# Splitting the next group's x earlier in the last second layer, and turning the keys right behind a unit's result

## The chip, the cores and the metric

The kernel runs on one core of a Trainium2 chip. The metric is the device time of one execution in microseconds (us); the time of the kernel before is 1023.07 us, the median of three runs from 1022.1 to 1024.09.

## The reference

Two blocks run one after the other. The first is a gated linear recurrence over 4 batches, 8 heads, 768 positions and head dimension 48; its output, with the heads side by side, is the input x of a mixture of 4 experts:

```
state = alpha[t] * state + k[t] v[t]^T          # per batch and head, 48 x 48
y[t]  = q[t] state
x = y, (4 * 768) x (8 * 48)                     # 3072 rows of 384
p = domain_probs / (sum of domain_probs + 1e-9)
out = sum over e of p[:, e] * (max(x @ w1[e], 0) @ w2[e])     # w1: 384 x 1024, w2: 1024 x 384
```

## The kernel before

**Units and groups.** A unit is one chunk of 128 positions of one batch: 6 chunks times 4 batches, 24 units. The recurrence of a unit is a generator, `attention(u)`, with 17 steps (counted here from 0). The units' outputs are gathered into groups of rows for the experts: group 0 has 2 units, groups 1 to 5 have 4 each, group 6 the last 2. Units 2 to 5 make group 1, 6 to 9 group 2, 10 to 13 group 3, 14 to 17 group 4, 18 to 21 group 5.

**The MoE.** For each group and expert, `up` (the first layer, called 8 times, once for each 128 columns of the hidden layer) and then `down` (the second layer). From group 1 on, a product of float32 numbers is made from three parts of each operand (in the code: top, low and dif), so that `up` of one column block takes 9 matmuls of 128x512 (L775) and `down` of a full group 96 matmuls of 128x384 (L852). These 96 steps go through two of the parts first (64 steps) and then through the third part slot by slot, a slot being one unit's 128 rows. When a slot's last matmul has been issued, `add_up` adds its PSUM result into an SBUF accumulator (L880 on ACT for the first expert, L882 on DVE for the others). The PSUM tiles of `up` ("one") and of `down` ("ops") share one tag, g, with four buffers.

**The parts of x.** ACT copies a unit's output from PSUM into `x_raw` (L675). During the last `down` of a group, `split_x` makes the parts of the next group's x: its step 0 makes the top part on ACT (L734), its steps 1 to 3 make low (L271) and dif (L805) on DVE for one third of the 384 input columns each. `down` runs these four steps from the list `between`, each when its matmul index has reached a given share of the steps. `split_x` for the two-unit group 6 runs in group 5's first expert, in smaller pieces.

**The hidden parts.** `up` makes the top hidden part on ACT (L777) and the low one on DVE (L800); `down` makes dif (L805) at every fifth step, eight times.

**The order.** All is issued by hand, in one program order, and each engine works through its own instructions in that order. Attention steps are dealt out between the matmuls of the MoE: `deal` gives each unit a stretch of a planner's clock, `BEATS` or `IN_PAIRS` (units 11 to 17) say at which share of the stretch each of the 17 steps falls, and `advance` runs the steps that are due while `up` and `down` count the clock up by `cost`. Two units are always in progress. For units in pairs, `TOGETHER` puts step 15 of a unit at the time of step 7 of the next one, and step 16 at step 11. Step 7 makes the score products (L567, tiles of 128x64).

**The end of a unit.** From unit 2 on, step 14 is `turn_keys`: four PE transposes of the last key tile into a PSUM tile (L287, called from L683) and an ACT copy into the tile AT (L683). It does nothing for the last chunk of a batch, units 20 to 23. Step 15 is `result`: PE products into a PSUM tile "yps" (L662, column strips of 32) and the ACT copy L675. Step 16 multiplies the turned keys by the values (L697) and updates the state on DVE (L707, L708). The key tiles of all units come from one pool with five buffers; the PSUM tiles of the transposes, of the result and of the state product share one tag, w, with two buffers. From unit 10 on, the inputs a, k and q are transposed on DVE (L488) instead of PE, so that the transposes L287 of these units are those of `turn_keys` alone.

Of the kernel before, what the change touches and what calls it, by code (L numbers as in the profile page):

```python
# [20 lines left out]
def kernel(  # L21
# [94 lines left out]
    half = B // 2  # L116
# [47 lines left out]
    in_runs = 10  # L164
# [10 lines left out]
    def load(u, names):  # L175
        if u >= len(units):
            return
        cb, b = units[u]
        for nm in names:
            src = srcs[nm][b, :, cb * P:(cb + 1) * P, :].rearrange("h s d -> s h d")  # L180
            if u == in_runs and nm != "v":
                nc.gpsimd.memset(runs_of[nm][:, :, RUN - HD // 4:], 0.0)
            for g in range(P // QUAD if u >= in_runs and nm != "v" else 0):
                i, tail = divmod(g, 2)
                off, n = (QUAD, RUN - HD // 4) if tail else (0, RUN)
                runs = srcs[nm][b].rearrange("(a i) s d -> i a (s d)", i=2)[
                    i, :, cb * P * D:(cb + 1) * P * D].rearrange("a (t n) -> t a n", t=QUAD)
                nc.sync.dma_start(out=runs_of[nm][QUAD * g:QUAD * (g + 1), :, :n],
                                  in_=runs[:, :, off:off + n])
            if u >= in_runs and nm == "a":  # L190
                continue
            nc.sync.dma_start(out=raw(u, nm)[:, :, :D], in_=src)
# [13 lines left out]
    def load_piece(l, i, beside=False):  # L206
        if i >= E * NQ * LAST:
            return
        gi, k = divmod(i, E * NQ)
        e, c = divmod(k, NQ)  # L210
        if gi > l and not (l == 1 and fresh(gi, e)):
            w = wt[l][i] = wts.tile([P, 3, KC * QF], F32R, name=f"w{l + 1}",
                                    bufs=AHEAD if l == 0 else NQ)
            nc.sync.dma_start(out=w.bitcast(F32), in_=kept[l][k])
            return
        if l == 1 and gi == 0 and not beside:
            return
        if l == 0:

            if e == 0:  # L220
                shared[c] = wts.tile([P, 3, KC * QF], F32R, name="w2", bufs=NQ)
            w = shared[c][:, 2 - e % 2].bitcast(F32)
        else:

            if gi > 1 or gi == 1 and e > 0:
                if c == 0:
                    shared["w2"] = hid.tile([P, NQ, KC * QF], F32, name="hT", bufs=NQ)
                w = shared["w2"][:, c]
            else:
                w = hidden[c][:, gi].rearrange("p f n -> p (f n)")[:, :KC * QF].bitcast(F32)  # L230
        wt[l][i] = w
        if l == 0:
            nc.sync.dma_start(
                out=w.rearrange("p (c f) -> p c f", f=QF),
                in_=moe_w1[e].rearrange("(c p) f -> p c f", p=P)[:, :, c * QF:(c + 1) * QF])
        else:
            nc.sync.dma_start(
                out=w.rearrange("p (c d) -> p c d", d=DM),
                in_=moe_w2[e].rearrange("(c p) d -> p c d", p=P)[:, c * FPQ:(c + 1) * FPQ])
# [34 lines left out]
    def norm_probs():  # L274
        nc.vector.reduce_sum(out=tot, in_=p_all, axis=AX.X)
        nc.vector.tensor_scalar_add(out=tot, in0=tot, scalar1=1e-9)
        nc.vector.reciprocal(out=tot, in_=tot)
        nc.vector.tensor_mul(p_all, p_all, tot.unsqueeze(2).broadcast_to([P, NBLK, E]))
# [197 lines left out]
    def attention(u):  # L476
# [206 lines left out]
                nc.scalar.copy(out=AT, in_=turned(lambda p: KT[:, p, :]))  # L683


        for step in (turn_keys, result) if u >= half else (result, turn_keys):
            step()
            yield

# [30 lines left out]
    def split_x(gi, step):  # L720

        n = len(groups[gi]) * P
        if step == 0 and gi < LAST:
            xTs[gi] = work.tile([P, 3, KC, NT], F32R, name="xT", bufs=1)
        elif step == 0:

            xTs[gi] = [work.tile([P, NP, P], F32R, name="KT", bufs=5) for _ in range(5)]
        for kc in range(KC) if step == 0 else [step - 1]:
            parts = [x_part(gi, part, kc) for part in range(3)]
            pieces = [(xraws[gi][:, kc, :n], parts)] if gi < LAST else                 [(raw[:, kc, :], [part[:, s * P:(s + 1) * P] for part in parts])  # L730
                 for s, raw in enumerate(xraws[gi])]
            for x, out in pieces:
                if step == 0:
                    nc.scalar.activation(out=out[0], in_=x, func=ACT.Copy, scale=TRIM)  # L734
                else:
                    split_rest(x, out)
# [159 lines left out]
    def cost(layer, gi, e):  # L896
        n = len(groups[gi]) / 4
        if layer == 0:
            return 2.1 * n if gi > 0 else 2.6 * n
        return 4.1 if gi > 0 else 5.4  # L900
# [50 lines left out]
    def advance(spent):  # L951
        nonlocal clock
        clock += spent
        while waiting and clock >= waiting[0][0]:
            next(waiting.popleft()[2], None)

    with tc.manual_schedule():
        nc.scalar.dma_start(out=ident_all, in_=nc.inline_tensor(ident_np, name="ident_c").ap())
        nc.scalar.dma_start(out=masks_all, in_=nc.inline_tensor(mask_np, name="masks_c").ap())
        nc.gpsimd.memset(sts[B - 1], 0.0)  # L960
        for nm in "akq":
            for r in (early[nm], apart[nm]):
                nc.gpsimd.memset(r[:, :, D:], 0.0)
        nc.gpsimd.memset(lat[HALF:, :, :HALF], 0.0)
        for t in values + blocks:
            nc.gpsimd.memset(t, 0.0)
        for t in sts[:-1]:
            nc.gpsimd.memset(t, 0.0)

        load(0, "aqkv")  # L970
        load(1, "akqv")
        for i in range(NQ):
            load_piece(0, i)

        idle = ps.tile([P, DM], F32, name="idle", tag="g", bufs=4)
        zeros = sts[B - 1].rearrange("p a i d -> p (a i d)")

        def fill(times, n=P):  # L980
            for _ in range(times):
                nc.tensor.matmul(idle[:, :n], lhsT=zeros[:, :P], rhs=zeros[:, :n], start=True, stop=True)

        runs = [None, attention(1)]
        fill(7)
        runs[0] = first_unit(fill, runs[1])
        nc.sync.dma_start(out=p_all, in_=moe_domain_probs.rearrange("(n p) e -> p n e", p=P))

        span = cost(0, 0, 0) * FCH / 2 + cost(1, 0, 0)
        waiting.extend((span * (k + 1) / 15, u, runs[u])  # L990
                       for k, u in enumerate([1, 1, 1, 0, 1, 0, *[1] * 8]))
        for fc in range(FCH):
            up(0, 0, fc, slice(0, 1))
            if fc == FCH // 2:
                norm_probs()
            advance(cost(0, 0, 0) / 2)
        down(0, 0, [0], deque())
        while waiting:
            next(waiting.popleft()[2], None)
        clock = 0.0  # L1000
        waiting.extend((1.0 + k, 1, runs[1]) for k in range(2))
        waiting.extend(deal())

        for (gi, e), after in zip(tasks, [*tasks[1:], (None, None)]):
            rest = gi == e == 0
            for fc in range(FCH):
                up(gi, e, fc, slice(1, len(groups[0])) if rest else None)
                advance(cost(0, gi, e) / (2 if rest else 1))
            each = len(groups[gi]) if gi > 0 else 1
            turns = [range(k, k + each) for k in range(rest, len(groups[gi]), each)]  # L1010
            for k, slots in enumerate(turns):

                between = deque()
                if after[1] == 0:

                    for step, at in enumerate((0.0, 0.3, 0.42, 0.54) if gi == 0 else
                                              (0.0, 0.6, 0.7, 0.78)):
                        at = at * len(turns) - k
                        if 0 <= at < 1:
                            between.append((at, lambda step=step: split_x(after[0], step)))  # L1020
                down(gi, e, slots, between)
        while stores:
            stores.popleft()()
# [28 lines left out]
```

## Time and profile before

The profiled execution took 1022.68 us, of which 1020.8 us are the span that the profile covers.

| what | before |
|---|---|
| median of three runs | 1023.07 us |
| the profiled execution | 1022.68 us, span 1020.8 us, mean granted clock 0.994 |
| L852, second layer, 2112 matmuls | 377.8 us busy |
| L775, first layer, 1440 matmuls of 128x512 | 344.3 us busy |
| L271 and L805 on xT, 15 each | 10.3 and 10.4 us busy |
| L683, copies of turned keys, 19 | 11.1 us busy, 582 ns each |
| L882, sums of a slot, 66 | 39.7 us busy |

The last second layers of groups 1 to 5 begin, by the timeline of PE, at 309.08, 474.97, 632.31, 796.95 and 833.58 us from the start of the span, and the next group's first layer begins at 330.15, 492.06, 651.93, 815.32 and 850.22 us. (That of group 5 is that of its first expert.)

How to read the profile: times count from the start of the span. A row of a timeline gives the start, the length, the engine, the line, the operation, what is written and read, the shape and the number of instructions merged into it, and in brackets how long the engine was idle before it and what ended that. A row of waits gives the waiting engine and line, what it waited for, the sum, the number and the longest. A row of busy times by stretch gives for each engine the busy time and the number of instructions, then the granted share of the TensorE clock (PEclk) and the DMA load. A chain lists the pieces of work that released one another, in order of time.

### The profile page before, as it was taken

What the parts mean: (1) busy time and instruction counts of PE and PEld (TensorE: products, weight loads), DVE (VectorE), ACT (ScalarE), POOL (GpSimd) and SP (SyncE); (2) the same over time, 40 slices, a digit from 0 to 9 for tenths busy, and PEclk for the clock granted to TensorE, in tenths of its full rate; (3) what the DMA queues carried; (4) which work ended last, traced back from release to release, by engine and by line L of the source; (5) the groups of instructions that cost most, each with busy time, mean ns of one, the idle gap of its engine ahead of it and who ended that gap; (6) DMA issues with size and microseconds to landing.
All of it is one profiled execution on the core that took longest, in us unless ns stands there. A gap on an engine that the chain in (4) does not pass through costs nothing.

```text
span 1020.8 us, 21134 instructions
## 1 busy us (share of the span) xinstructions
PE 998.8 (98%) x8564; PEld 888.5 (87%) x8564; DVE 701.0 (69%) x1430; ACT 438.5 (43%) x961; POOL 36.1 (4%) x79
## 2 busy tenths in 40 slices
PE   8889999999999999999999999999999999999998
PEld 7767777989888799898898898898988989899998
DVE  5698869676999768677767666886786742434333
ACT  4677765364354444335443415444454232111111
POOL 2010000000000100000000000000000000000000
PEclk9999999999999999999999999999999999999999
DMA  9499699478989799789889759887796445453531
GB/s 209 132 383 292 201 317 356 152 285 279 348 292 293 279 298 329 292 248 321 287 259 339 230 216 376 271 283 286 211 368 238 165 200 190 182 204 167 226 146 47
DMA packets 155632, 260.19 MB, mean 255 GB/s; under 512 B 95216, under 2 KB 132464, under 8 KB 133520
## 3 DMA queue, kind: packets, MB, share of 16 engines
q1 hardware_dynamic: 149072, 216.44, 63.6%
q0 software_dynamic: 6016, 42.08, 10.2%
q8 instruction: 68, 1.11, 0.4%
q10 hardware_dynamic: 448, 0.33, 0.1%
q14 instruction: 28, 0.23, 0.1%
HBM read 216.35 MB, written 42.47 MB: 254 GB/s over the span
## 4 chain that ended last, share of the span: by engine, by line
PE 83%; DVE 11%; ACT 3%; issue 2%; DMA 0%; SPq 0%; DVEq 0%; ACTq 0%
PE ops L852 35%; PE one L775 32%; PE sc L567 5%; PE yps L662 3%; PE one L769 2%; PE tp L287 2%; DVE w L252 1%; ACT qb L541 1%; DVE hT L800 1%; PE sps L697 1%; DVE QT L548 1%; DVE near L577 1%; DVE w L253 1%; PE far L623 1%; DVE hT L805 1%
## 5 line engine op out<-in xcount | busy, mean ns | idle before, releaser
L852 PE MATMUL ops<-w,hT 128*128 128x384 f32 x2112 | 377.8, 338 | 1.2 <-DVE hT L800 1.2
L852 PEld LDWEIGHTS ops<-w,hT 128*128 128x128 f32 x2112 | 365.2, 188 | 4.5 <-DVE hT L800 2.0
L775 PE MATMUL one<-xT,w 128*128 128x512 f32 x1440 | 344.3, 395 | 3.7 <-DVE acc L882 3.6
L775 PEld LDWEIGHTS one<-xT,w 128*128 128x128 f32 x1440 | 267.7, 188 | 62.0 <-DVE acc L882 4.6
L777 ACT ACTIVATE hT<-one 128x512 fp32r<-128x512 f32 (+1 forms) x192 | 108.0, 562 | 342.2 <-PE one L775 325.2
L800 DVE SCALAR_TENSOR_TENSOR hT<-one,hT 128x512 fp32r<-128x512 f32 (+1 forms) x192 | 122.0, 644 | 101.9 <-ACT hT L777 101.6
L541 ACT COPY qb<-QT 64x256 f32<-64x256 f32 x322 | 131.2, 407 | 98.3 <-DVE QT L518 45.0
L548 DVE TENSOR_TENSOR QT<-QT,AT 128x256 f32<-128x256 f32 x158 | 66.5, 421 | 79.2 <-ACT qb L541 78.2
L805 DVE SCALAR_TENSOR_TENSOR hT<-hT 128x512 fp32r<-128x512 f32 (+1 forms) x192 | 111.7, 639 | 0.1
L577 DVE COPY_PREDICATED near<-masks,sc 128x256 f32<-128x256 uint8 x138 | 73.8, 535 | 43.7 <-PE sc L567 40.4
L567 PEld LDWEIGHTS sc<-qb,KT 128*64 128x64 f32 x2208 | 69.7, 138 | 7.9 <-issue 6.3
L567 PE MATMUL sc<-qb,KT 128*64 128x64 f32 x2208 | 74.0, 223 | 1.5 <-ACT qb L541 0.8
L882 DVE SCALAR_TENSOR_TENSOR acc<-ops,p_all,acc 128x384 f32<-128x384 f32 x66 | 39.7, 614 | 42.2 <-PE ops L852 42.2
L560 DVE TENSOR_TENSOR KT<-KT,AT 128x256 f32<-128x256 f32 x161 | 67.4, 419 | 1.6 <-PE sc L567 1.6
L559 ACT COPY KT<-KT 128x256 f32<-128x256 f32 x138 | 57.4, 416 | 3.4
L769 PE MATMUL one<-xT,w 128*128 128x256 f32 (+1 forms) x240 | 47.4, 346 | 0.4 <-ACT xT L460 0.4
L852 PE MATMUL ops<-hT 128*128 128x384 f32 x128 | 46.2, 494 | 0.0
L769 PEld LDWEIGHTS one<-xT,w 128*128 128x128 f32 x240 | 38.5, 194 | 5.2 <-ACT xT L460 0.6
L550 DVE TENSOR_TENSOR AT<-AT 128x256 f32<-128x256 f32 (+1 forms) x138 | 39.2, 284 | 4.7
L891 POOL DMA_DIRECT2D out_dram<-acc x22 | 11.9, 541 | 675.7 <-DVE acc L882 675.7
L775 PE MATMUL one<-KT,w 128*128 128x256 f32 x288 | 34.6, 279 | 0.0
L662 PE MATMUL yps<-lat,rv 128*32 128x128 f32 x736 | 33.1, 273 | 1.4 <-ACT lat L640 1.4
(119 smaller groups left out, 711.8 us busy)
## 6 DMA issues: line engine op xcount, KB each, us to landing
w<-kept SPq DMA_DIRECT2D x140, 1152.0 KB, 8.7
kept<-w POOLq DMA_DIRECT2D x32, 1152.0 KB, 9.1
hT<-in_moe_w_dram SPq DMA_DIRECT2D x36, 384.0 KB, 5.8
w<-in_moe_w_dram SPq DMA_DIRECT2D x16, 384.0 KB, 6.1
rv<-in_v_dram SPq DMA_DIRECT2D x24, 192.0 KB, 9.0
out_dram<-acc POOLq DMA_DIRECT2D x22, 192.0 KB, 5.8
rk<-in_k_dram SPq DMA_DIRECT2D x14, 192.0 KB, 6.1
rq<-in_q_dram SPq DMA_DIRECT2D x14, 192.0 KB, 3.0
```

What stands on the lines that cost most here:

```text
L541: nc.scalar.copy(out=qb[rows, :, i, :].rearrange("p a (b r) -> p a b r", r=m), in_=qv[rows])
L548: nc.vector.tensor_mul(qv, qv, spread(dv[:, :, :, 0], m))
L560: nc.vector.tensor_mul(new[:, :, :, 0, :], old[:, :, :, 0, :], spread(halved(decs[li])[:, :, :, 1], m))
L567: nc.tensor.matmul(out[HALF * s:HALF * (s + 1), 2 * p:2 * p + 2, :], lhsT=KTs[li][:, p, HALF * s:HALF * (s + 1)], rhs=qbs[li][:, p, :, QUA ...
L577: nc.vector.copy_predicated(near.rearrange("p a (b two r) -> p a b two r", two=2, r=m)[:, :, :, 1, :], mk.unsqueeze(1).broadcast_to([P, H, ...
L662: nc.tensor.matmul(yps[QUAD * j:QUAD * (j + 1), c, :], lhsT=lhsT, rhs=rhs, start=begins, stop=ends)
L769: nc.tensor.matmul(one, lhsT=w[:, kc], rhs=xraws[gi][:, kc, lo:hi], start=(kc == 0), stop=(kc == KC - 1))
L775: nc.tensor.matmul(one, lhsT=w[:, part, kc], rhs=x_part(gi, part, kc), start=(part == 1 and kc == 0), stop=(part == 0 and kc == KC - 1))
L777: nc.scalar.activation(out=parts[0], in_=one, func=ACT.Relu, scale=TRIM)
L800: nc.vector.scalar_tensor_tensor(out=low, in0=x, scalar=0.0, in1=top.bitcast(F32), op0=ALU.max, op1=ALU.subtract)
L805: nc.vector.scalar_tensor_tensor(out=dif, in0=low.bitcast(F32), scalar=-4096.0, in1=top.bitcast(F32), op0=ALU.mult, op1=ALU.add)
L852: nc.tensor.matmul(sums[slot], lhsT=h, rhs=w, start=(n == begins[slot]), stop=(n == ends[slot]))
```

## The change

Two things change. The list of shares at which the steps of `split_x` run in the last `down` goes from 0.0, 0.6, 0.7, 0.78 to 0.0, 0.42, 0.5, 0.58 for every group but group 0, whose shares stay. And from unit 10 on (`in_runs` is 10), step 14 does nothing, and step 15 runs `result` and then `turn_keys` in one go; units before the tenth keep their order. The number of steps and their times stay. For units 20 to 23 nothing changes, since `turn_keys` does nothing there and `result` stays in step 15.

```diff
@@ attention @@
-        for step in (turn_keys, result) if u >= half else (result, turn_keys):
+        joined = u >= in_runs
+        if joined:
+            yield
+            result()
+        for step in (turn_keys,) if joined else (turn_keys, result) if u >= half else (result, turn_keys):
             step()
             yield
@@ the loop over tasks @@
                     for step, at in enumerate((0.0, 0.3, 0.42, 0.54) if gi == 0 else
-                                              (0.0, 0.6, 0.7, 0.78)):
+                                              (0.0, 0.42, 0.5, 0.58)):
                         at = at * len(turns) - k
                         if 0 <= at < 1:
                             between.append((at, lambda step=step: split_x(after[0], step)))
```

## The prediction

> **What bounds the kernel.** I read the page first, then the waits of PE, the busy time and granted clock by stretch around the last second layer of each group, the chain of waits there, and the timelines of DVE, ACT and PE.
>
> ```profile
> PE 998.8 (98%) x8564; PEld 888.5 (87%) x8564; DVE 701.0 (69%) x1430; ACT 438.5 (43%) x961; POOL 36.1 (4%) x79
> ```
>
> PE is the bound over the span: whatever makes it stand longer, or gives it more to do, is added to the end. DVE has slack on average only. The waits of PE name where it stands:
>
> ```profile
> engine line waited for: us in total, times, longest us
> PE one L775 <- DVE acc L882: 3.6, 2, 2.5
> ...
> PE ops L852 <- DVE hT L800: 1.2, 2, 1.0
> ```
>
> The first two waits stand where one group ends and the next begins: 2.54 us before 330.15 (group 1 to 2) and 1.10 us before 651.93 (group 3 to 4). There the first matmul of the next first layer needs a PSUM buffer of tag g that the sum of slot 0 (L882, on DVE) still reads. The long one has a sequel:
>
> ```profile
> core 0: us, PE busy (x) PEld busy (x) DVE busy (x) ACT busy (x) POOL busy (x), PEclk, DMA share, GB/s
> ...
> 326.20:329.60 3.40, 1.41 (x9) 1.09 (x7) 3.30 (x8) 1.57 (x4) 0.00 (x0) 1.00 0.97 238
> 329.60:333.00 3.40, 2.85 (x7) 2.27 (x8) 3.22 (x7) 0.00 (x0) 2.04 (x4) 0.50 1.03 378
> ...
> 650.45:653.85 3.40, 2.30 (x11) 1.34 (x10) 3.33 (x7) 1.33 (x3) 0.54 (x1) 1.00 0.88 314
> ```
>
> After a stretch of 3.40 us with PE busy for 1.41 (58% idle) the clock is halved for the next 3.4 us; a stretch with 32% idle, the third row, leaves it whole. The half clock costs (333.00 - 330.15) / 2 = 1.43 us. The clock records of this trace change only at multiples of 3.413 us from each other; stretches on that raster with 58 and 60% idle lost the clock, one with 50% kept it (an early one, among transposes, lost it with 42%). I take 1.85 us idle inside one stretch as the point.
>
> **Part 1, the x parts earlier.** A last second layer has 96 matmul steps. The three pairs of split instructions (L271, then L805) move from steps 58, 68 and 75 to 41, 48 and 56 (0.6, 0.7, 0.78 and 0.42, 0.5, 0.58 of 96, rounded up). They stay on DVE; no instruction is added, and no DMA moves. What counts is what they now stand ahead of in DVE's queue: the sum of slot 0, issued behind step 71 in groups 2 to 5 (64 steps of parts 0 and 1, then 8 for a slot) and behind step 77 in group 1 (where two of a slot's eight come first for all slots). So in group 1 all three pairs are ahead of it both before and after; in groups 2, 3 and 4 the third pair stood behind it and now stands ahead. One pair takes 1.32 us (491.42 to 492.74 below).
>
> *Group 3 to 4.* The chain runs through DVE without a break:
>
> ```profile
> 650.02 0.61 DVE xT L271
> 650.64 0.02 issue
> 650.66 0.69 DVE xT L805
> 651.35 0.54 DVE acc L882
> 651.89 0.04 issue
> 651.93 2.30 PE one L775 x8
> ```
>
> DVE is busy for 17.68 of the 18.06 us from 633.84 to 651.90 (its busy time by stretch), so nothing absorbs the pair: L882 ends 1.32 later, PE starts at 653.25. Before, PE then lost some 0.2 us on the third pair (x part 1 of the last third is the third matmul's input); that goes. Net +1.1 us, and the wait grows from 1.10 to 2.42.
>
> *Group 2 to 3.* No wait before; the DVE and PE timelines show how narrow it is:
>
> ```profile
> 489.56 0.68 DVE L271 TENSOR_TENSOR xT<-x_raw,xT 128x512 fp32r<-128x512 f32 x1
> 490.28 0.69 DVE L805 SCALAR_TENSOR_TENSOR xT<-xT 128x512 fp32r<-128x512 f32 x1
> 490.89 0.61 DVE L882 SCALAR_TENSOR_TENSOR acc<-ops,p_all,acc 128x384 f32<-128x384 f32 x1
> 491.42 0.68 DVE L271 TENSOR_TENSOR xT<-x_raw,xT 128x512 fp32r<-128x512 f32 x1
> 492.13 0.69 DVE L805 SCALAR_TENSOR_TENSOR xT<-xT 128x512 fp32r<-128x512 f32 x1
> 492.74 0.61 DVE L882 SCALAR_TENSOR_TENSOR acc<-ops,p_all,acc 128x384 f32<-128x384 f32 x1
> ```
>
> ```profile
> 485.89 0.60 PE L287 MATMUL tp<-ident,KT 128*128 128x128 f32 x4
> 486.25 5.97 PE L852 MATMUL ops<-w,hT 128*128 128x384 f32 x33
> 492.06 2.24 PE L775 MATMUL one<-xT,w 128*128 128x512 f32 x9
> ```
>
> L882 of slot 0 ends at 491.50, PE wants its buffer at 492.06. With the third pair ahead it ends at 492.82 (DVE is busy for 15.95 of the 16.26 us from 475.80 to 492.06), so PE starts 0.8 later. Part 2 also takes unit 14's four transposes out of this layer: PE comes 0.45 sooner, only to wait 1.25 instead.
>
> *Group 1 to 2.* The same instructions stand ahead of slot 0's sum, and DVE is busy for 20.56 of 20.90 us (309.20 to 330.10): wait and half clock stay. *Group 4 to 5:* L882 would end at 813.8, PE wants it at 815.32: nothing. *Group 5 to 6:* DVE is idle from 843 to 852: nothing.
>
> Earlier splits make attention steps of DVE (copies into QT, KT, the masked takes) up to 4 us later. Who waits for them are ACT's copies (2.7 to 8.4 us idle ahead of the next L777) and the products and results of the next first layer, 2 us or more later: nothing. If that cover were gone, each would cost what is missing of 1.3 us.
>
> **Part 2, turns behind the result.** Only units 10 to 19 turn keys at all (20 to 23 are last chunks). Four transposes inside matmuls of the MoE cost PE 0.45 us: 96 steps with them took 492.06 - 474.97 = 17.09, without 850.22 - 833.58 = 16.64. So there is no cost of interruption to save; the work just moves.
> - Units 10, 17 and 19 get matmuls of the MoE behind the turns. Starts in the trace: 0.20 us from the result's last matmul to the next full-width one, 3 x 0.109 inside the transposes, 0.03 from there to the MoE, and 0.09 extra on the second matmul, where a return from a result costs 0.11. Added 0.33, removed 0.45: -0.12 each.
> - Units 11 to 16 and 18 get the next unit's products, of 128x64 tiles, right behind. Result to products takes 0.20; now result to transposes 0.20, inside 0.33, and transposes to products, which the trace does not show: between 0.03 (to a full-width matmul) and 0.22 (to the first unit's 64x32 tiles); I take 0.20, measured to L458's small tiles, the nearest. Added 0.53, removed 0.45: +0.08 each, with ends of -0.1 and +0.1.
> - Sum: 7 x 0.08 - 3 x 0.12 = +0.2. Of unit 14's removed 0.45 nothing is gained, as shown: +0.45.
>
> On ACT the copy of the turned keys (582 ns) now stands ahead of the next unit's L559; behind them the next L777 had waited 3.50 us for PE in the joint turn at 536 to 540, which hides it. On DVE the KT write of the next unit (L560) comes to wait for the transposes, since it takes over the buffer that they read; DVE stood there 5.29 us for the products anyway. The state update that needs the turned keys is at least one first-layer chunk (2.1 us) later. Each would cost up to 0.6 us a unit without that cover.
>
> One gain: unit 10's copy (582 ns, starting 339.35) leaves ACT's queue ahead of the qb copy for which DVE waits 3.73 us until 340.67. DVE then runs unbroken to PE's wait of 1.03 us for L800 at 356.98. DVE 0.47 earlier: -0.47, less the -0.12 of unit 10, which is then hidden.
>
> **Sum.** 2 to 3: +0.8 +0.45; 3 to 4: +1.1; turns +0.3 (unit 10's gain now hidden); wait at 357: -0.47. Together +2.2 us. Then the clock: a 2.42 us wait puts at least 1.85 us into one stretch of 3.41 for (3.41 - 1.85 + 2.42 - 1.85) / 3.41 = 62% of its positions. That is the likelier, and by the row at 330 costs 1.4: +3.6. The profiled execution took 1022.68 us (span 1020.8 and 1.9 around it), 0.4 below the median of 1023.07; 1022.68 + 3.6 = **1026.3 us**.
>
> **Rivals.**
> - *The clock stays whole* (27%): all as above without the drop, 1024.9. For it: 38% of the positions, and the wait may come out shorter. The Trainium skill, "TensorE: Matmul & The Clock Gate", HAM oscillation, says that idle gaps over some 3.4 us bring the clock down; by it 2.42 us are harmless and the sum would be this one. The row at 330, half clock after 2.54 us, speaks against the rule as it stands.
> - *DVE absorbs the pair* (15%): if L882 slips by 0.6 or less, group 2 to 3 loses nothing, 3 to 4 at most 0.6, and the turns near 0: 1023.2. Against it: 0.3 to 0.4 us idle in both stretches.
> - *Faster* (10%): the place is 327.6 to 333.0. Splits started sooner let DVE reach slot 0's sum at least 0.7 us sooner there (its busy time would have to hold hidden waiting); from there the wait falls under 1.85 and the half clock goes: -0.7 - 1.43, down to -4.0 for all, and the other two borders lose nothing for the same reason: 1018.7 to 1020.5. Against it: the same queue ahead, 98% busy.
> - *The change does nothing* is part of the second rival: were the third pair to land behind the sum still, only the turns would be left.
>
> My forecast has 48%. Runs of this kernel can tell 0.2%, some 2.05 us, from no change. Slower by more: nearly all of the forecast (46) and 16 of the first rival's 27, 62%; within: the rest, 28%; faster: 10%. The range runs from 1022.7 (second rival with its turns at their low end) to 1027.6 (the forecast, turns at their high end, a whole half-clock stretch of 1.7): it leaves out the faster case and little above.
>
> **What would show it.** Right: L882 after three split pairs at the end of groups 2 and 3; PE's wait for it near 1.2 us at group 2 to 3 and 2.4 at 3 to 4; a stretch at half clock behind the latter; an unchanged wait of 2.5 at 1 to 2; the wait for L800 near 0.6. Wrong: DVE idle in those stretches, or a wait at 1 to 2 that has shrunk.

## The result and the profile after

The changed kernel takes 1026.35 us, the median of six runs from 1024.74 to 1028.93; the kernel before took 1022.59 us in six runs beside them (1020.8 to 1024.13). The ratio is 1.0038 with a 95% interval from 1.002 to 1.0057: 3.8 us slower. The profiled execution took 1025.26 us with a span of 1023.4. Four lines were added, so L775 is now L779, L800 L804, L805 L809, L852 L856 and L882 L886.

PE has the same work as before, to 0.2 us, in a span 2.6 us longer (page, busy time of the changed kernel):

```profile
PE 998.6 (98%) x8564; PEld 887.2 (87%) x8564; DVE 701.9 (69%) x1430; ACT 439.3 (43%) x961; POOL 36.1 (4%) x79
```

The waits of PE say where it stood (waiting line, releaser, sum, number, longest):

```profile
engine line waited for: us in total, times, longest us
PE one L779 <- DVE acc L886: 6.0, 3, 2.5
...
PE ops L856 <- DVE hT L804: 0.8, 2, 0.6
```

Three waits for a slot's sum in place of two, 6.0 us in place of 3.6. DVE's timeline at the border of group 2 to 3 shows the cause:

```profile
489.63 0.69 DVE L271 TENSOR_TENSOR xT<-x_raw,xT 128x512 fp32r<-128x512 f32 x1
490.35 0.69 DVE L809 SCALAR_TENSOR_TENSOR xT<-xT 128x512 fp32r<-128x512 f32 x1
490.96 0.42 DVE L548 TENSOR_TENSOR QT<-QT,AT 128x256 f32<-128x256 f32 x1
...
491.94 1.14 DVE L886 SCALAR_TENSOR_TENSOR acc<-ops,p_all,acc 128x384 f32<-128x384 f32 x2
```

The third split pair (489.63) now stands ahead of slot 0's sum; before, it stood behind that sum and ahead of slot 1's (rows 490.89 to 492.74 in the prediction). With nothing left between them, the two sums show as one row, 491.94. (The attention step at 490.96 stood ahead of slot 0's sum before, too.) PE's timeline has the answer at all three borders, each row with the idle time ahead of it:

```profile
329.32 3.87 PE L779 MATMUL one<-xT,w 128*128 128x512 f32 x9 [2.52 <-DVE acc L886]
...
492.61 2.34 PE L779 MATMUL one<-xT,w 128*128 128x512 f32 x9 [1.10 <-DVE acc L886]
...
654.71 5.51 PE L779 MATMUL one<-xT,w 128*128 128x512 f32 x23 [2.42 <-DVE acc L886]
```

The wait is 2.5 us as before at 1 to 2, 1.10 where there was none at 2 to 3, and 2.42 in place of 1.10 at 3 to 4.

The two profiles must be laid side by side with care. The profile of before had a half-clock stretch at 15.6 us, long before anything differs, and the one after had not: the changed kernel is 0.82 us ahead when it reaches the change and 2.61 behind from 718 us on. The change cost 3.43 us in this profile, without any drop of the clock at 3 to 4.

### The profile page after: what moved, and what is told of

Its sections match the earlier page's. It is cut to its first block, busy times and chain, and to the rows that moved or that the text cites. A ratio compares the mean times of both kernels' runs of the same rounds, so it can differ in the third digit from the quotient of the medians.

```text
span 1023.4 us, 21133 instructions
## 1 busy us (share of the span) xinstructions
PE 998.6 (98%) x8564; PEld 887.2 (87%) x8564; DVE 701.9 (69%) x1430; ACT 439.3 (43%) x961; POOL 36.1 (4%) x79
## 4 chain that ended last, share of the span: by engine, by line
PE 80%; DVE 13%; ACT 3%; issue 3%; DMA 0%; SPq 0%; DVEq 0%; ACTq 0%
PE ops L856 33%; PE one L779 32%; PE sc L567 5%; PE yps L662 3%; PE one L773 2%; PE tp L287 2%; DVE hT L809 2%; DVE w L252 1%; DVE hT L804 1%; ACT qb L541 1%; DVE QT L548 1%; PE sps L701 1%; DVE near L577 1%; PE far L623 1%; DVE w L253 1%
## 5 line engine op out<-in xcount | busy, mean ns | idle before, releaser
L856 PE MATMUL ops<-w,hT 128*128 128x384 f32 x2112 | 376.0, 337 | 1.0 <-DVE hT L804 0.8
L856 PEld LDWEIGHTS ops<-w,hT 128*128 128x128 f32 x2112 | 365.5, 188 | 4.5 <-DVE hT L804 1.7
L779 PE MATMUL one<-xT,w 128*128 128x512 f32 x1440 | 343.8, 395 | 6.1 <-DVE acc L886 6.0
L779 PEld LDWEIGHTS one<-xT,w 128*128 128x128 f32 x1440 | 268.1, 189 | 63.9 <-DVE acc L886 7.3
L804 DVE SCALAR_TENSOR_TENSOR hT<-one,hT 128x512 fp32r<-128x512 f32 (+1 forms) x192 | 122.0, 645 | 101.5 <-ACT hT L781 101.1
L809 DVE SCALAR_TENSOR_TENSOR hT<-hT 128x512 fp32r<-128x512 f32 (+1 forms) x192 | 111.7, 639 | 0.1
L886 DVE SCALAR_TENSOR_TENSOR acc<-ops,p_all,acc 128x384 f32<-128x384 f32 x66 | 39.5, 614 | 41.5 <-PE ops L856 41.5
L856 PE MATMUL ops<-hT 128*128 128x384 f32 x128 | 46.2, 494 | 0.0
L779 PE MATMUL one<-KT,w 128*128 128x256 f32 x288 | 34.6, 279 | 0.0
```

The source lines that it names most:

```text
L779: nc.tensor.matmul(one, lhsT=w[:, part, kc], rhs=x_part(gi, part, kc), start=(part == 1 and kc == 0), stop=(part == 0 and kc == KC - 1))
L804: nc.vector.scalar_tensor_tensor(out=low, in0=x, scalar=0.0, in1=top.bitcast(F32), op0=ALU.max, op1=ALU.subtract)
L809: nc.vector.scalar_tensor_tensor(out=dif, in0=low.bitcast(F32), scalar=-4096.0, in1=top.bitcast(F32), op0=ALU.mult, op1=ALU.add)
L856: nc.tensor.matmul(sums[slot], lhsT=h, rhs=w, start=(n == begins[slot]), stop=(n == ends[slot]))
```

## The experiments

The theory: what costs is the place of the third split pair in DVE's queue, ahead of slot 0's sum, for which PE waits; a long wait may take the clock with it. Rival "turns": the joined turns of the keys cost most of it. Rival "earliness": earlier splits delay attention on DVE, and that costs. All edits are against the kernel before unless they say otherwise; experiments 1 to 4 ran beside 23 runs of it, median 1023.04 us, the others beside 9, median 1023.13.

**1. The split shares alone.**

```diff
-                                              (0.0, 0.6, 0.7, 0.78)):
+                                              (0.0, 0.42, 0.5, 0.58)):
```

> The split shares of the change alone; step order of the units as before. Queue theory (what costs is that the third split pair stands ahead of slot 0's sum on DVE at two group borders): the wait at group 2 to 3 is about 0.8 us (not 1.1, since unit 14's transposes are still in that layer), at 3 to 4 about 2.4, at 1 to 2 still 2.5; 2.1 us slower than before without a drop of the clock behind the 2.4 us wait, 3.5 with one, so +2 to +3.5 in the median. Rival 'turns' (the joined turns cost most of it): within 1 us of before, waits as before.

Measured: 1026.81 us, ratio 1.0042 (1.003 to 1.0054), +3.8 us. PE's timeline at 2 to 3 and 3 to 4:

```profile
494.36 1.89 PE L775 MATMUL one<-xT,w 128*128 128x512 f32 x7 [0.68 <-DVE acc L882]
655.66 1.65 PE L775 MATMUL one<-xT,w 128*128 128x512 f32 x3 [2.42 <-DVE acc L882]
```

0.68 and 2.42 us, as the theory said; the second row runs three matmuls in 1.65 us, so here the clock fell. Against the kernel before, this profile loses 0.94 us around 2 to 3, 1.32 in the wait at 3 to 4 and 1.28 in the matmuls behind it. The rival "turns" (the turns cost most of it) is refuted: none are joined here, and the loss is as large. It isn't the same loss, though. Without the clock it is 2.3 us here and 3.4 in the changed kernel, which leaves some 1.1 for the turns; the drop behind the 2.42 us wait makes up the difference in this profile. The total lies a little above the +2 to +3.5 expected; all six runs had a mean granted clock of 0.992 or 0.993, those of the changed kernel 0.992 to 0.998.

**2. The joined turns alone** (the first hunk of the change, old shares).

```diff
+        joined = u >= in_runs
+        if joined:
+            yield
+            result()
```

> The joined turns alone; split shares as before. Queue theory: no wait at 2 to 3, 1.1 us at 3 to 4, 2.5 at 1 to 2; what is left are the turns themselves, by the trace of the changed kernel +0.14 us for a unit whose turns are followed by products, some +0.4 where the wait for the hidden dif parts eats what unit 11's removal saves, -0.3 at the wait for L800: about +1 us in all. Rival 'turns': +3 us or more.

Measured: 1023.85 us, ratio 1.0004 (0.9994 to 1.0014): not told apart from before. The profile can: waits for the sums of 2.5 and 1.1 us at the same borders as before, and 1.1 us lost against the kernel before between 310 us and 718 us (1.44 to 2.53 us behind), as expected.

**3. Early pairs, third pair behind the sum.**

```diff
-                                              (0.0, 0.6, 0.7, 0.78)):
+                                              (0.0, 0.42, 0.5, 0.78)):
```

> The kernel before with the first two split pairs as early as in the change (0.42 and 0.5) and the third where it was (0.78), so behind slot 0's sum in groups 2 to 5. Queue theory: waits as before (2.5, none, 1.1), time within 0.5 us of before. Rival 'earliness' (the delay of attention's DVE steps by earlier splits is what costs): two thirds of the loss of the splits, +1.4 to +2.3 us.

Measured: 1023.45 us, ratio 1.0008 (1 to 1.0017), +0.4 us. In the profile the distance to the kernel before is 1.49 us ahead of the first of these layers and 1.51 at 750 us: two pairs moved by 17 and 20 matmuls cost nothing. "Earliness" is refuted; of the three moves, only the third one's, past the sum, costs.

**4. Third pair one slot later.** In group 1 it comes behind slot 0's sum; no other place in the order changes.

```diff
-                                              (0.0, 0.6, 0.7, 0.78)):
+                                              (0.0, 0.6, 0.7, 0.82)):
```

> The kernel before with the third pair at 0.82 instead of 0.78: on DVE this moves one pair in group 1 behind slot 0's sum, and nothing else. Queue theory: the wait at 1 to 2 falls from 2.5 to 1.2 us, so the clock stays whole there: -1.3 from the wait and -1.4 from the clock in the runs that had the drop, 2 to 2.7 us faster. Rival 'earliness': later x parts make the first layer wait for them instead, no gain or slower. Page's rule of 3.4 us idle for the clock: only the 1.3.

Measured: 1019.62 us, ratio 0.9966 (0.9953 to 0.9979): 3.4 us faster than before, with one number changed. The border of group 1 to 2 in the kernel before, DVE and PE:

```profile
328.15 0.68 DVE L271 TENSOR_TENSOR xT<-x_raw,xT 128x512 fp32r<-128x512 f32 x1
328.87 0.69 DVE L805 SCALAR_TENSOR_TENSOR xT<-xT 128x512 fp32r<-128x512 f32 x1
329.48 1.14 DVE L882 SCALAR_TENSOR_TENSOR acc<-ops,p_all,acc 128x384 f32<-128x384 f32 x2
...
330.15 3.65 PE L775 MATMUL one<-xT,w 128*128 128x512 f32 x9 [2.54 <-DVE acc L882]
```

DVE's timeline there with the third pair later:

```profile
326.76 0.69 DVE L805 SCALAR_TENSOR_TENSOR xT<-xT 128x512 fp32r<-128x512 f32 x1
327.37 0.61 DVE L882 SCALAR_TENSOR_TENSOR acc<-ops,p_all,acc 128x384 f32<-128x384 f32 x1
327.90 0.68 DVE L271 TENSOR_TENSOR xT<-x_raw,xT 128x512 fp32r<-128x512 f32 x1
328.61 0.69 DVE L805 SCALAR_TENSOR_TENSOR xT<-xT 128x512 fp32r<-128x512 f32 x1
```

PE's, at the same place:

```profile
328.03 2.52 PE L775 MATMUL one<-xT,w 128*128 128x512 f32 x9 [1.19 <-DVE acc L882]
```

The sum (327.37) now precedes the third pair, the wait falls from 2.5 to 1.19 us, and nine matmuls take 2.52 us in place of 3.65: the half-clock stretch is gone. Against the kernel before the profile gains 1.34 in the wait and 1.13 in the nine matmuls behind it, 2.5 us in all, within the 2 to 2.7 expected. The 3.4 us between the medians are more; their interval reaches from 2.1 to 4.8, and the rest isn't traced to a cause. (In this profile the clock also stayed whole at 67 us, far ahead of the edit, where the profile of before lost it.) The later pair is in time for PE.

**5. Two pairs behind the sum, top part first.**

```diff
+            parts_in_order = (0, 1, 2) if fc == 0 and e == 0 else (1, 2, 0)
-            for part in (1, 2, 0):
+            for part in parts_in_order:
...
-                                              (0.0, 0.6, 0.7, 0.78)):
+                                              (0.0, 0.6, 0.82, 0.82)):
```

> The kernel before with the second and third pair both at 0.82, which puts two pairs behind slot 0's sum at every border; and, since they then come late, the first block of an expert-0 first layer takes the top part of x first, then low and dif. Queue theory: no wait for slot 0's sum at 1 to 2 and 3 to 4 (one pair less each than in the kernel with 0.82 for the third alone); some 0.6 to 1 us of waiting for xT or for slot 1's sum in its place at 1 to 2, 0.5 at 3 to 4; 3 to 4 us faster than before, level with or 0.9 better than that kernel. Rival 'earliness': the wait for xT takes all of it back, no better than that kernel or worse.

Measured: 1019.12 us, ratio 0.9964 (0.9952 to 0.9977), the fastest median, and not told apart from experiment 4. PE's waits:

```profile
PE ops L854 <- DVE hT L802: 1.2, 2, 1.0
PE one L776 <- DVE xT L271: 1.0, 2, 0.5
```

No wait for a sum at the borders is left; 0.5 us of waiting for x parts twice stands in its place. The profiles can: this one is 0.59 us behind that of experiment 4 at 306 us, ahead of these borders, and 0.45 ahead at 692, so 1.0 us is gained at the borders 1 to 2 and 3 to 4.

**6. The changed kernel with the third pair of group 4's x done twice** (the second time the same values are written).

```diff
-                    split_rest(x, out)
+                    for _ in range(2 if (gi, step) == (4, 3) else 1):
+                        split_rest(x, out)
```

> The changed kernel with the third split pair of group 4's x done twice (the same values written again), so that one pair more stands ahead of slot 0's sum at 3 to 4. Queue theory: the wait there goes from 2.4 to 3.75 us, +1.3 us; and, since 3.75 us put 1.87 us or more into one 3.41 us stretch wherever they fall, the clock drops behind it every time, +1.4 over runs of the changed kernel without a drop: 1.3 to 2.7 us slower than the changed kernel, the profile with a half-clock stretch at 655 to 660. If DVE had room, no change.

Measured: 1029.5 us in four runs (1026.96 to 1031.55), ratio to the kernel before 1.0058 (1.0036 to 1.0081), 3.2 us over the changed kernel's median, above the 1.3 to 2.7 expected. PE's timeline at 3 to 4:

```profile
658.14 4.46 PE L780 MATMUL one<-xT,w 128*128 128x512 f32 x12 [3.87 <-DVE acc L887]
```

The wait is 1.45 us longer for one pair more, and the clock falls at 659.39: against the first profile of the changed kernel, which kept its clock there, this one loses 1.45 us in the wait and 1.6 in the matmuls behind it. That the clock falls in every run isn't shown: the fastest of the four had a mean granted clock of 0.997, and no profile was taken of it.

**7 and 8. The changed kernel again**, two single runs.

> The changed kernel itself once more. Waits 2.5, 1.1 and 2.4 us as in its first profile, to some 0.05 us; whether the clock drops behind the last one depends on where it falls on the 3.413 us raster, by the estimate of the prediction in 62% of the cases.

> As the other repetition of the changed kernel: same waits, the drop behind the wait at 3 to 4 in about 62% of the cases, and the time of the profiled execution 1.3 to 1.5 us longer with it than without, counted from the wait on.

Measured: 1026.12 and 1025.28 us; waits of 2.52 and 2.55 us at 1 to 2, 1.10 and 2.42 in both. Behind the 2.42 us, the first kept its clock and the second lost it. Busy time and granted clock by stretch of the raster, for the first:

```profile
651.59:655.00 3.41, 1.54 (x9) 1.22 (x8) 3.31 (x9) 2.46 (x7) 0.00 (x0) 1.00 0.88 191
655.00:658.41 3.41, 2.86 (x13) 2.39 (x14) 3.13 (x7) 2.19 (x5) 1.55 (x3) 1.00 0.98 379
```

and for the second:

```profile
649.54:652.96 3.42, 1.00 (x7) 0.69 (x5) 3.35 (x9) 2.45 (x8) 0.00 (x0) 1.00 0.80 168
652.96:656.37 3.41, 3.41 (x8) 2.73 (x9) 2.57 (x6) 1.13 (x2) 2.11 (x4) 0.50 1.01 382
```

The same wait leaves 1.87 us idle in one stretch (3.41 - 1.54) where the raster cuts it, and 2.42 where it doesn't. The second lost 1.6 us in the layer behind the wait that the first did not, a little above the 1.3 to 1.5 expected. Its whole time is shorter even so: it had no half-clock stretch in the first 70 us, the first had two, and it was 2.6 us ahead when it came to the wait.

## Why the prediction was right, and where its terms were off

**The mechanism** held at every border. Whether the third pair stands behind or ahead of slot 0's sum is the whole effect of part 1 (experiments 1 and 3, and 4 the other way round); at 1 to 2 nothing changed, at 2 to 3 PE waited 1.10 us (1.25 forecast), at 3 to 4 2.42 (2.42 forecast), at 4 to 5 and 5 to 6 nothing. PE's starts, compared border by border in the two profiles, give the sizes:

| step of the sum | forecast, us | measured, us |
|---|---|---|
| wait at 1 to 2 | 0 | 0 |
| wait for L800 at 357, unit 10's gain in it | -0.47 | -0.28 |
| unit 11 | +0.08 | +0.55 |
| units 12, 13, 15, 16, each | +0.08 | +0.14 |
| group 2 to 3 | +0.8 | +0.82 |
| unit 14, turns and the removal that gains nothing | +0.53 | +0.69 |
| unit 17 | -0.12 | -0.07 |
| group 3 to 4 | +1.1 | +1.13 |
| units 18 and 19 together | -0.04 | +0.03 |
| sum without the clock | +2.2 | +3.4 |
| clock behind the 2.42 us wait | +1.4 | none here; 1.3 in experiment 1, 1.6 in 8 |

The borders came out as forecast. Of the 1.2 us that the sum fell short without the clock, 1.0 is the joined turns with their side effects (units 11 to 19) and 0.2 the smaller gain at 357.

**The turns** were mis-sized. The two transitions that the trace of before did not show were read rightly: 0.20 us from the result to the transposes and 0.20 from the transposes to the products, in the changed kernel's starts. What the sum left out is inside: behind the result's 32-column strips the second transpose starts 0.165 us after the first, where inside full-width matmuls it started after 0.109. So a joined unit pays 0.59 for 0.45.

**Unit 11** is the largest miss. The prediction credited its removed 0.45 us, with nothing late next. The changed kernel's timeline shows what was late:

```profile
355.89 11.67 PE L856 MATMUL ops<-w,hT 128*128 128x384 f32 x65 [0.64 <-DVE hT L804]
367.72 4.25 PE L856 MATMUL ops<-w,hT 128*128 128x384 f32 x23 [0.16 <-DVE hT L809]
```

Without the transposes PE reaches the third part of the second layer sooner and waits for the hidden dif (L809), 0.60 us from start to start where 0.17 is usual. The prediction had seen this trap for unit 14, where the sum of slot 0 sets the end, and not for unit 11. The first row also shows the wait for L800 that was to shrink by 0.47: 1.03 to 0.64.

**Group 3 to 4** lost 1.32 us in the wait, and 0.19 came back in the matmuls behind it, where 0.2 was forecast: before, the third, fourth and seventh of them started late while DVE still made the third pair (651.80 to 653.20).

**The clock** was the step with the least ground. The sum took the drop as the likelier case, by 62% of positions. Of four profiles with a wait of 2.42 us (the change three times, experiment 1) two had it, and the first profile of the change hadn't: it went the way of the rival "the clock stays whole", 1025.26 us for 1024.9. The point of 1.85 us idle didn't hold either, since 1.87 us left the clock whole in experiment 7. So the sum of 3.6 us stood on 2.2 and a full drop, and the measured 3.8 us are 3.4 and a drop in part of the runs (in one of the three profiles). That the totals agree so well is luck: a term that was too small and one that was too large made up for each other. The Trainium skill's rule in "TensorE: Matmul & The Clock Gate", HAM oscillation, that idle gaps over some 3.4 us bring the clock down, did not hold here as a bound: waits of 2.42 us did it twice, and one of 2.5 us at 1 to 2 in each profile of the kernel before and of the change. The free-running window of 3.413 us that the Trainium skill gives on that page, Part 1, agrees with the raster in these traces.

**The rivals.** "DVE absorbs the pair" is refuted by the waits. "Faster" named the right place: at 1 to 2, 1.3 us less wait takes the half clock with it. But it takes moving a pair behind the sum, not moving pairs forward, as experiment 4 shows.

## What to carry to other kernels

When an engine's queue is full up to the moment that another engine needs its result, moving work earlier in that queue gains nothing by itself (experiment 3); what counts is what stands ahead of the one instruction that the other engine waits for. So put the release of a buffer ahead of preparations that are needed a little later, even if both are "for the next stage". And when an interruption costs no more than the work in it (here four transposes, 0.45 us alone), there is little to save by joining it to another: where full-width matmuls followed, units 17 and 19 gained 0.07 and 0.09 us, and where 128x64 tiles followed, units 12, 13, 15 and 16 lost 0.14 each. Ask what stands on both sides before merging.

## What the runs showed of the hardware that was not expected

The clock doesn't go by the length of a wait alone. Its records change at multiples of 3.413 us from each other in every profile, and this raster lies differently in each execution: the half-clock stretch behind 1 to 2 begins at 329.59 us in the kernel before and at 329.22 in the changed one. The same wait of 2.42 us falls on either side. In the two profiles that lost the clock one stretch held 2.20 and 2.42 us of idle time, in the two that kept it at most 1.22 and 1.87.

How much idle time in one stretch it takes isn't settled. Ahead of 330 us in the kernel before, 1.99 us (58%) lost the clock; in experiment 8, far ahead of these borders, 1.98 us (58%) left it whole:

```profile
62.45:65.86 3.41, 1.43 (x8) 0.92 (x6) 3.31 (x8) 2.02 (x5) 1.07 (x2) 1.00 1.02 386
65.86:69.28 3.42, 3.24 (x48) 2.81 (x50) 3.32 (x8) 3.19 (x8) 0.44 (x1) 1.00 1.10 419
```

And the early stretch with 42% idle that the prediction names lost it. So the idle time of PE in these views doesn't decide alone; what else does, no run here shows.

The six runs of the changed kernel go with their mean granted clock, from 1024.74 us at 0.998 to 1028.93 at 0.992. So do the 32 runs of the kernel before beside the experiments, from 1020.03 us at 0.998 to 1024.71 at 0.993. Most of the spread of this kernel thus seems to be the number of half-clock stretches (a reading of the mean clock, not of a profile of each run), and a gain of 1 us shows in a profile where six runs can't tell it.
